# Last output layer of a fused attention and two-layer-MLP kernel: six of seven token tiles as seven block products

## The chip, the cores and the metric

The kernel runs on one core of a Trainium2 chip. The metric is the device time of one execution in microseconds (us). The three timed runs of the kernel before took 1274.81, 1283.0 and 1287.9 us, so the median is 1283.0 us. One more execution was taken with the hardware profiler; all rows below are from it.

## The reference

Everything is float32. Talking-heads attention is followed by two MLPs, and the second one is what the change touches:

```python
h = x @ w_in                                   # x: 1792 x 768, w_in: 768 x 2048
r = np.maximum(h, 0.0)
g = r * r                                      # 1792 x 2048
return (g @ w_out).astype(np.float32)          # w_out: 2048 x 768
```

The last output layer is the product `g @ w_out` for the second half of the tokens: 896 tokens, 2048 hidden features, 768 outputs.

## The kernel before

**Stages.** Attention writes its result in four token blocks of 448 to memory. Then the two MLPs run for two halves of 896 tokens each. The order of the stages in `run` is: first MLP of the first half (`inner(0)`, `outer_first`), second MLP of the first half (`inner(1)`, `outer_last(0)`), and then for the second half `seven(0)` (first input layer), `outer_combos` (first output layer), `seven(1)` (second input layer) and `outer_last(1)` (second output layer, the end of the program).

**How a float32 product is made.** Each operand is split into a high part (ScalarE casts it, `wh`, `xh`, `rh`, `eh`) and a low part (VectorE subtracts the high part from the operand, `wl`, `xl`, `rl`, `el`). `three` (L664 to L666) then issues three matmuls: high times high, high times low, low times high. L664 needs only the two high parts.

**Block products.** `seven` and the stages before it already use a scheme with seven block products where the plain one has eight: a 2x2 block matrix product is made from seven products of sums of blocks. In `seven` the sums of weights come from `combine` on VectorE, in products named b11, t1, b21, b22, t2, t3, t4. Eight groups `q` of seven products make the stage; `late` and `close` put the two last elementwise steps of a result some products later. `outer_last` does not use the scheme.

**outer_last(1).** h (the squared ReLU) lies in 16 tiles `hr` of 128 features by 896 tokens. For each of two halves `nh` of 384 outputs and each of 16 feature tiles `f` the stage takes one weight tile of 128x384 and issues `three` for seven token tiles: 2 x 16 x 7 x 3 = 672 matmuls with 384 moving columns, into seven PSUM banks. `split_ahead` splits a whole `hr` tile of 896 columns two steps ahead, in each half again (32 splits); `Weights.next` splits the weight tile of a step three steps ahead. After each half seven copies, by VectorE and ScalarE in turn, go to SBUF tiles `tmp` and are stored by SyncE.

**outer_combos.** Two passes `t` over 16 steps `f`. A step issues 18 matmuls of 448 columns. VectorE and ScalarE split one `hr` tile (L670, L669) and one weight tile (L525, L518) in a step. In the last three steps of a pass the matmuls are ordered by output tile, so that the results of the pass can be split while the matmuls still run.

**What sets the order.** The program is written out by hand: each engine runs its instructions in the order in which the Python code issues them, and a wait holds up everything behind it on that engine. All weight loads and stores are issued by SyncE in one such order. `Weights.units` is the list of weight tiles in order of use; `load_ahead` loads up to six tiles ahead into six buffers `wf` (four more are named `aq`), and `part` splits one tile into one of five buffer pairs `wh`, `wl`. The splits of h use four buffer pairs `rh`, `rl`. PSUM has eight banks, which `bank` hands out in turn.

Of the kernel before, what the change touches and what calls it, by code (L numbers as in the profile page):

```python
# [16 lines left out]
B, H, S, D = 4, 12, 448, 64  # L17
# [5 lines left out]
KC, FC = DM // 128, DFF // 128  # L23
WU = 448
FU = DM // 2
LINE = 256
MOVING, STATIONARY = 128, 224
# [354 lines left out]
class Weights:  # L382
# [180 lines left out]
def col(i):  # L563
    return slice(i * 128, (i + 1) * 128)


class Mlps:
    BLOCKS = [slice(j * S, (j + 1) * S) for j in range(2)]

    def __init__(self, tc, ctx, dram, psum, xd, weights, out):  # L570
        self.tc, self.nc, self.ctx, self.psum, self.xd, self.out = tc, tc.nc, ctx, psum, xd, out
        self.weights = Weights(tc.nc, dram, *weights)
        self.banks = 0
        self.pending = []
# [157 lines left out]
    def seven(self, m, x, carry=()):  # L732
# [23 lines left out]
        for q in range(FC // 2):  # L756
            a, b, c, d, e = (self.bank()[:, :S] for _ in range(5))
            plan = (("b11", a), ("t1", b), ("b21", a), ("b22", b), ("t2", c), ("t3", d), ("t4", e))
            for i, (name, p) in enumerate(plan):
# [81 lines left out]
    def outer_first(self, xh, xl, hh, hl):  # L841
        nc = self.nc
        for o in range(KC):
# [11 lines left out]
            for j, bl in enumerate(self.BLOCKS):  # L855
                self.split(xh[:, o, bl], xl[:, o, bl], p[j])

    def outer_combos(self):

        nc, tt, w = self.nc, self.nc.vector.tensor_tensor, self.weights  # L860
# [7 lines left out]
        for t in range(2):  # L868
            p = [[self.bank()[:, :S] for _ in self.BLOCKS] for _ in range(3)]
            taken = []  # L870
            for f in range(FC):
                s = t * FC + f
                tail = f >= FC - 3
# [61 lines left out]
    def outer_last(self, half):  # L935
# [27 lines left out]
                nc.sync.dma_start(out=self.out[r : r + 128, nh * n2 : (nh + 1) * n2], in_=o)  # L963
        return x if half == 0 else None

    def run(self):
        with ExitStack() as ctx:
            hp = self.pool("hp", "left", ctx)
# [19 lines left out]
        self.seven(0, x)  # L988
        x, carry = self.outer_combos()
        self.hr = {}  # L990
        self.start_split(STATIONARY)
        self.seven(1, x, carry)
        self.outer_last(1)


# ---- launch: one core; the host only lays the arrays out
# [46 lines left out]
```

## Time and profile before

| what | us |
|---|---|
| median of three timed runs (lowest, highest) | 1283.0 (1274.81, 1287.9) |
| time of the profiled execution | 1277.57 |
| its span, first to last instruction | 1275.7 |
| TensorE (PE) busy in the span | 1233.7 (97%) |
| VectorE (DVE) busy | 943.1 (74%) |
| ScalarE (ACT) busy | 679.3 (53%) |

In the rows below a time stamp is in us from the start of the span. In a row of the timeline the first number is the start, the second the duration of the instruction (or of all of them, where "xN" ends the row). A matmul's recorded duration overlaps the next one, so the pitch of matmuls is read from their starts. PEld is the weight load of TensorE, L12 is line 12 of the kernel, and square brackets give the idle time of the engine just before and the instruction that ended it.

### The profile page before, as it was taken

What the parts mean: (1) busy time and instruction counts of PE and PEld (TensorE: products, weight loads), DVE (VectorE), ACT (ScalarE), POOL (GpSimd) and SP (SyncE); (2) the same over time, 40 slices, a digit from 0 to 9 for tenths busy, and PEclk for the clock granted to TensorE, in tenths of its full rate; (3) what the DMA queues carried; (4) which work ended last, traced back from release to release, by engine and by line L of the source; (5) the groups of instructions that cost most, each with busy time, mean ns of one, the idle gap of its engine ahead of it and who ended that gap; (6) DMA issues with size and microseconds to landing.
All of it is one profiled execution on the core that took longest, in us unless ns stands there. A gap on an engine that the chain in (4) does not pass through costs nothing.

```text
span 1275.7 us, 35064 instructions
## 1 busy us (share of the span) xinstructions
PE 1233.7 (97%) x14295; PEld 1101.7 (86%) x14296; DVE 943.1 (74%) x1974; ACT 679.3 (53%) x1476; POOL 52.4 (4%) x118
## 2 busy tenths in 40 slices
PE   9999989999789999999999999999999999999998
PEld 4677777777579999988899999999999998999998
DVE  4577667777759998778999996868874559887452
ACT  4666666666537774333444554546663445454342
POOL 1011010110410000000000000000000000000000
PEclk9999999999999999999999999999999999999999
DMA  6666646555635545666666555131221111212131
GB/s 186 201 204 195 208 161 205 185 171 184 203 108 177 174 155 162 191 184 199 224 222 227 186 174 171 49 119 50 69 75 55 51 50 50 75 44 85 34 105 44
DMA packets 124121, 179.02 MB, mean 140 GB/s; under 512 B 25177, under 2 KB 103353, under 8 KB 123961
## 3 DMA queue, kind: packets, MB, share of 16 engines
q1 hardware_dynamic: 123720, 176.50, 43.0%
q8 instruction: 112, 1.84, 0.6%
q14 instruction: 49, 0.39, 0.1%
q10 hardware_dynamic: 240, 0.29, 0.1%
HBM read 101.86 MB, written 36.18 MB: 108 GB/s over the span
## 4 chain that ended last, share of the span: by engine, by line
PE 76%; DVE 11%; ACT 6%; DMA 3%; issue 3%; SPq 0%; ACTq 0%; DVEq 0%; POOL 0%; POOLq 0%
PE ps_qk L664 5%; PE ps_qk L666 5%; PE ps_qk L665 5%; PE ps_pv L665 5%; PE ps_pv L666 5%; PE ps_pv L664 5%; PE ps_post L664 5%; PE ps_post L666 5%; PE ps_post L665 5%; PE ps_mix L664 5%; PE ps_mix L666 5%; PE ps_mix L665 5%; PE ps_mix L182 4%; PE ps_post L218 4%; PE ps_pv L254 3%; PE ps_qk L156 3%
## 5 line engine op out<-in xcount | busy, mean ns | idle before, releaser
L518 ACT CAST wh<-wf 128x384 fp32r<-128x384 f32 (+1 forms) x272 | 133.3, 492 | 209.6 <-DVE wf L477 129.4
L525 DVE TENSOR_TENSOR wl<-wf,wh 128x384 fp32r<-128x384 f32 (+1 forms) x272 | 144.7, 534 | 76.4 <-ACT wh L518 74.7
L218 PEld LDWEIGHTS ps_post<-wg,ex 60*64 60x64 f32 x5040 | 139.5, 135 | 51.2 <-issue 30.2
L192 ACT ACTIVATE ex<-ps_mix,nmax 128x448 f32<-128x448 f32 x180 | 112.6, 630 | 117.5 <-DVE nmax L190 117.4
L670 DVE TENSOR_TENSOR rl<-hr,rh 128x896 fp32r<-128x896 f32 x96 | 104.5, 1089 | 54.4 <-ACT rh L669 54.4
L218 PE MATMUL ps_post<-wg,ex 60*64 60x60 f32 x5040 | 135.0, 220 | 6.5 <-issue 4.9
L236 DVE COPY at<-ps_post 128x420 f32<-128x420 f32 x178 | 97.6, 591 | 53.8 <-PE ps_post L218 51.1
L182 PE MATMUL ps_mix<-graw,pre 64*64 64x448 f32 (+1 forms) x720 | 113.6, 557 | 13.8 <-ACT ex L192 6.3
L190 DVE TENSOR_REDUCE nmax<-ps_mix 128x1 f32<-128x448 f32 x180 | 104.5, 616 | 24.3 <-PE ps_mix L182 23.9
L669 ACT CAST rh<-hr 128x896 fp32r<-128x896 f32 x96 | 90.1, 939 | 50.3 <-PE ps_post L666 25.1
L254 PE MATMUL ps_pv<-at,v 64*64 64x110 f32 (+3 forms) x2976 | 100.0, 249 | 5.3 <-issue 2.9
L254 PEld LDWEIGHTS ps_pv<-at,v 64*64 64x64 f32 x2976 | 88.4, 134 | 14.9 <-issue 6.5
L156 PE MATMUL ps_qk<-kt,qt 64*64 64x448 f32 (+1 forms) x680 | 92.6, 543 | 1.5 <-ACT sc L161 1.2
L447 ACT ACTIVATE wf<-wd 128x384 f32<-128x384 f32 (+1 forms) x134 | 68.1, 512 | 42.8 <-DMA wd<-w1o 24.0
L161 ACT COPY sc<-ps_qk 120x448 f32<-120x448 f32 x167 | 80.7, 539 | 11.1 <-PE ps_qk L156 11.1
L477 DVE SCALAR_TENSOR_TENSOR wf<-wd,wf 128x384 int32<-128x384 int32 (+1 forms) x134 | 67.7, 509 | 3.9
L475 DVE SCALAR_TENSOR_TENSOR wf<-wd,wf 128x384 int32<-128x384 int32 (+1 forms) x134 | 67.7, 509 | 3.8
L182 PEld LDWEIGHTS ps_mix<-graw,pre 64*64 64x64 f32 (+1 forms) x720 | 34.7, 134 | 32.7 <-ACT ex L192 16.6
L684 ACT ACTIVATE tmp<-tmp 128x448 f32<-128x448 f32 x48 | 27.9, 581 | 57.2 <-DVE tmp L794 43.9
L664 PE MATMUL ps_qk<-xh,wh 128*128 128x448 f32 x150 | 55.3, 369 | 0.3 <-DVE tmp L691 0.3
L666 PE MATMUL ps_qk<-xh,wl 128*128 128x448 f32 x150 | 55.0, 367 | 0.0
L665 PE MATMUL ps_qk<-xl,wh 128*128 128x448 f32 x150 | 55.0, 367 | 0.0
(247 smaller groups left out, 3152.1 us busy)
## 6 DMA issues: line engine op xcount, KB each, us to landing
graw<-sc SPq DMA_DIRECT2D x180, 210.0 KB
wd<-w1i SPq DMA_DIRECT2D x32, 384.0 KB
wd<-w1o SPq DMA_DIRECT2D x48, 256.0 KB
wd<-w2i SPq DMA_DIRECT2D x32, 384.0 KB
wf<-w2of SPq DMA_DIRECT2D x48, 192.0 KB
wd<-w2o SPq DMA_DIRECT2D x22, 384.0 KB
w1if<-wf SPq DMA_DIRECT2D x32, 192.0 KB
w1of<-wf SPq DMA_DIRECT2D x48, 128.0 KB
```

The costliest lines, as they stand in the source:

```text
L156: nc.tensor.matmul(out[a][x:y], qt[n][o, p, x:y], k[o, p, :], start=True, stop=True)
L182: nc.tensor.matmul(out[r][64 * g : 64 * g + 64], pre64[o], e[g][o], start=True, stop=True)
L190: nc.vector.tensor_reduce(nmax, p, AX.X, ALU.max, negate=True)
L192: nc.scalar.activation(e, p, AF.Exp, bias=nmax, scale=1.0, accum_out=tot[s][:, r : r + 1])
L218: nc.tensor.matmul(out[g][y, 6 if c == 3 else 2 * c + r], e[rows][o, key : key + 64], w[o, rows], start=True, stop=True)
L254: nc.tensor.matmul(p, vt[b, i // 3][y, jc, g % 6 * D : (g % 6 + 1) * D], m, start=(jc == 0), stop=(jc == JC - 1), skip_group_check=True)
L518: self.nc.scalar.copy(hi, f)
L525: self.nc.vector.tensor_tensor(lo, self.single.pop(i), hi.bitcast(F32), ALU.subtract)
L664: mm(p, wh, xh, start=first, stop=False)
L665: mm(p, wh, xl, start=False, stop=False)
L666: mm(p, wl, xh, start=False, stop=last)
L670: self.nc.vector.tensor_tensor(lo, raw, hi.bitcast(F32), ALU.subtract)
```

## The change

The end of the program, `outer_last(1)`, becomes `seven_last`.

- Of the seven token tiles, tiles 0 to 2 and 4 to 6 form the two row blocks; the 2048 features and the 768 outputs are cut into two blocks each. Seven products `n` of eight steps `f`, each with three token tiles, replace the plain ones. Token tile 3 is left out of the scheme: its two halves of outputs are accumulated beside products 0, 2 and 3 in two more banks (`rest`). A step has 15 matmuls in product 0, 12 in products 2 and 3 and 9 in products 1, 4, 5 and 6: 8 x (15 + 9 + 12 + 12 + 9 + 9 + 9) = 600 matmuls of 384 columns.
- The sums of h (`sums`, and in place in `hr`) are made by VectorE, one of 128x384 in each step of products 0 to 3, in the room of the tile `xh`. `part_last` splits 512 or 384 columns of one tile three steps ahead, 56 times. The first three splits lie in the last group of `seven(1)`, behind products 2, 4 and 6 of it; before, two splits of 896 columns lay behind products 2 and 4.
- The sums of weights are made in `outer_combos` by `sum_weights`: for each of eight feature tiles four loads of 128x384 by SyncE, four subtractions by VectorE (two in each of two steps, ahead of that step's splits), and four stores into a scratch tensor `w2ot`. Together that is 32 loads, 32 subtractions and 32 stores.
- The last stage takes 64 weight tiles instead of 32: 32 plain ones and 32 sums from the scratch. In a step it splits weight tiles until four are ready ahead.
- The results are combined after the products: six VectorE operations after each of products 4 and 5, three in product 6, plain copies elsewhere. The order of the last three steps of product 6 is by output tile.

```diff
@@ Weights: the list of tiles
-        self.units += kept
+        half = FC // 2
+        self.k2o, self.k2t = k2o, keep("w2ot", [4 * half, 128, FU])
+        place = {"b11": 0, "b21": half, "b12": FC, "b22": FC + half}
+        self.units += [("f32", k2o[place[x] + f], None, MOVING) for f in range(half) for x in ("b11", "b12")]
+        for x in ("t1", "b21", "b22", "t2", "t3", "t4"):
+            of = self.k2t[(int(x[1]) - 1) * half :] if x[0] == "t" else k2o[place[x] :]
+            self.units += [("f32", of[f], None, MOVING) for f in range(half)]
@@ seven
-                if q == FC // 2 - 1 and i in (2, 4):
-                    self.split_ahead(i // 4)
+                if q == FC // 2 - 1 and i in (2, 4, 6):
+                    if m == 0:
+                        if i < 6:
+                            self.split_ahead(i // 4)
+                    else:
+                        self.part_last(0, i // 2 - 1)
@@ new, called at the head of each step s of outer_combos
+    def sum_weights(self, s):
+        w, half, sub = self.weights, FC // 2, self.nc.vector.tensor_tensor
+        for j, at in enumerate((-1, 2, 4, 7, 10, 14, 18, 22)):
+            if s == max(at, 0):
+                self.four[j] = []
+                for x in (0, FC, half, FC + half):
+                    o = self.tmp()[:, :FU] if j in (1, 3) else w.plain("aq", 4)
+                    self.nc.sync.dma_start(out=o, in_=w.k2o[x + j])
+                    self.four[j].append(o)
+            if s == at + 2:
+                b11, b12, b21, b22 = self.four[j]
+                sub(b11, b12, b11, ALU.subtract)
+                sub(b12, b22, b12, ALU.subtract)
+            if s == at + 3:
+                b11, b12, b21, b22 = self.four.pop(j)
+                sub(b22, b22, b11, ALU.subtract)
+                sub(b21, b22, b21, ALU.subtract)
+                for i, o in enumerate((b11, b22, b12, b21)):
+                    self.nc.sync.dma_start(out=w.k2t[i * half + j], in_=o)
@@ new
+    def part_last(self, n, f):
+        a = (STATIONARY - H_AT) % LINE // 4
+        t = self.sums[f] if n in (1, 4) else self.hr[f + (FC // 2 if n in (2, 3, 6) else 0)]
+        t = t[:, 512:] if n == 6 else t[:, : 512 if n in (0, 2, 3) else 384]
+        parts = [self.hq.tile([128, 2 * S + LINE // 4], F32R, name=f"r{x}", bufs=4)[:, a : a + t.shape[1]] for x in "hl"]
+        self.split(*parts, t)
+        self.halves[n, f] = parts
@@ new, in place of outer_last(1); the core of its loop
+        for k, (n, f) in enumerate(steps):
+            w.load_ahead(w.used)
+            hi, lo = self.halves.pop((n, f))
+            if f == 0 and n in (1, 4, 5, 6):
+                banks.append([self.bank()[:, :FU] for _ in range(3)])
+            p = banks[(0, 1, 0, 1, 2, 3, 4)[n]]
...
+            if not tail:
+                for i in range(3):
+                    for g, hi, lo, weights in taken:
+                        self.three(p[i], hi[:, col(i)], lo[:, col(i)], *weights[0], n not in (2, 3) and g == 0,
+                                   n in (2, 3, 4, 5, 6) and g == half - 1, True)
...
+                if n in (0, 2, 3):
+                    for j, y in enumerate(weights):
+                        q = j if n == 0 else n - 2
+                        self.three(rest[q], hi[:, col(3)], lo[:, col(3)], *y, n == 0 and f == 0, n > 0 and f == half - 1, True)
...
+            while w.done < min(len(w.units), w.used + 4):
+                w.part()
+            if k + 3 < len(steps):
+                self.part_last(*steps[k + 3])
+            low, high = self.hr[f], self.hr[f + half]
+            if n == 0:
+                tt(self.sums[f], low[:, 512:], high[:, 512:], ALU.add)
+            elif n == 1:
+                tt(self.sums[f], self.sums[f], low[:, :FU], ALU.subtract)
+            elif n == 2:
+                tt(high[:, :FU], high[:, :FU], self.sums[f], ALU.subtract)
+            elif n == 3:
+                tt(low[:, :FU], low[:, :FU], low[:, 512:], ALU.subtract)
...
+                elif n == 4:
+                    tt(u[i], p[i], one_a[i], ALU.add)
+                    o = room()
+                    tt(o, both[i], u[i], ALU.add)
+                    put(o, i, 1)
```

Line numbers move with the change: L669 and L670 (the splits) become L675 and L676, L518 and L525 (the parts of weights) L524 and L531, L664 to L666 (the matmuls) L670 to L672.

Two places on VectorE matter below. The first is where the two passes of `outer_combos` meet. Rows of before; `xl` is the low part of a result of the first pass, `rl` that of an h tile for the second pass, `wl` that of a weight tile:

```order
L670 TENSOR_TENSOR xl<-ps_mix,xh 128x448
L889 TENSOR_TENSOR tmp<-tmp,ps_mix 128x448
L670 TENSOR_TENSOR xl<-tmp,xh 128x448
L670 TENSOR_TENSOR rl<-hr,rh 128x896 x2
L525 TENSOR_TENSOR wl<-wf,wh 128x384 x2
L670 TENSOR_TENSOR rl<-hr,rh 128x896
```

The same place in the change; `aq` are the weight tiles that are subtracted:

```order
L676 TENSOR_TENSOR xl<-ps_mix,xh 128x448
L921 TENSOR_TENSOR tmp<-tmp,ps_mix 128x448
L676 TENSOR_TENSOR xl<-tmp,xh 128x448
L880 TENSOR_TENSOR aq<-aq 128x384
L881 TENSOR_TENSOR aq<-aq 128x384
L676 TENSOR_TENSOR rl<-hr,rh 128x896 x2
L531 TENSOR_TENSOR wl<-wf,wh 128x384 x2
L884 TENSOR_TENSOR aq<-aq 128x384
L885 TENSOR_TENSOR aq<-aq 128x384
L676 TENSOR_TENSOR rl<-hr,rh 128x896
```

Two subtractions now stand between the last split of a result and the first split of h for the second pass, and two more behind the weight parts.

The second place is where `seven(1)` ends and the last stage begins. Rows of before; L793 to L801 and L753 combine the products of the last group, L693 squares the ReLU:

```order
L670 TENSOR_TENSOR rl<-hr,rh 128x896
L793 TENSOR_TENSOR tmp<-ps_post,tmp 128x448
L794 TENSOR_TENSOR tmp<-ps_mix,tmp 128x448
L525 TENSOR_TENSOR wl<-wf,wh 128x384
L800 TENSOR_TENSOR tmp<-ps_pv,tmp 128x448
L801 TENSOR_TENSOR tmp<-tmp 128x448
L525 TENSOR_TENSOR wl<-wf,wh 128x384
L753 TENSOR_TENSOR tmp<-tmp,ps_qk 128x448
L693 TENSOR_TENSOR hr<-tmp 128x448 x3
L525 TENSOR_TENSOR wl<-wf,wh 128x384 x2
L670 TENSOR_TENSOR rl<-hr,rh 128x896
```

The same place in the change (L799 to L807, L759 and L699 are the same lines as L793 to L801, L753 and L693); the row with L1069 is the first sum of h:

```order
L676 TENSOR_TENSOR rl<-hr,rh 128x512
L799 TENSOR_TENSOR tmp<-ps_post,tmp 128x448
L800 TENSOR_TENSOR tmp<-ps_mix,tmp 128x448
L531 TENSOR_TENSOR wl<-wf,wh 128x384
L806 TENSOR_TENSOR tmp<-ps_pv,tmp 128x448
L807 TENSOR_TENSOR tmp<-tmp 128x448
L531 TENSOR_TENSOR wl<-wf,wh 128x384
L676 TENSOR_TENSOR rl<-hr,rh 128x512
L759 TENSOR_TENSOR tmp<-tmp,ps_qk 128x448
L699 TENSOR_TENSOR hr<-tmp 128x448 x2
```

A split of 512 columns now stands ahead of L759. Behind the rows shown follow one more L699, four weight parts instead of two, a split of 512 columns and L1069.

## Rows read from the trace of the kernel before

**Rows 1.** The page's first line: span of the profiled execution.

```profile
span 1275.7 us, 35064 instructions
```

**Rows 2.** Windows of the last three stages: length, then busy us by engine (instructions), clock, DMA.

```profile
core 0: us, PE busy (x) PEld busy (x) DVE busy (x) ACT busy (x) POOL busy (x), PEclk, DMA share, GB/s
937.40:1053.00 115.60, 115.55 (x579) 108.10 (x578) 63.63 (x92) 53.35 (x86) 0.00 (x0) 1.00 0.20 59
1053.00:1155.20 102.20, 101.30 (x505) 94.36 (x504) 89.04 (x168) 53.82 (x111) 0.00 (x0) 1.00 0.19 59
1155.20:1272.00 116.80, 116.67 (x673) 116.34 (x672) 55.30 (x74) 44.20 (x68) 0.00 (x0) 1.00 0.20 62
```

**Rows 3.** Waits of TensorE from 830 us on: us in total, times, longest.

```profile
PE ps_mix L664 <- ACT tmp L775: 0.5, 1, 0.5
PE ps_post L664 <- ACT tmp L780: 0.4, 1, 0.4
```

**Rows 4.** Timeline, TensorE: end of the stage before, first and last matmul of the last stage.

```profile
1151.43 0.36 PE L666 MATMUL ps_post<-eh,wl 128*128 128x448 f32 x1
...
1155.03 0.36 PE L666 MATMUL ps_qk<-eh,wl 128*128 128x448 f32 x1
1155.23 0.34 PE L664 MATMUL ps_mix<-wh,rh 128*128 128x384 f32 x1
...
1271.53 0.34 PE L666 MATMUL ps_post<-wh,rl 128*128 128x384 f32 x1
```

**Rows 5.** Timeline, VectorE, where the last stage begins.

```profile
1151.36 1.08 DVE L670 TENSOR_TENSOR rl<-hr,rh 128x896 fp32r<-128x896 f32 x1
1152.37 0.61 DVE L793 TENSOR_TENSOR tmp<-ps_post,tmp 128x448 f32<-128x448 f32 x1
...
1155.68 0.61 DVE L753 TENSOR_TENSOR tmp<-tmp,ps_qk 128x448 f32<-128x448 f32 x1
1156.21 1.69 DVE L693 TENSOR_TENSOR hr<-tmp 128x448 f32<-128x448 f32 x3
1157.82 1.02 DVE L525 TENSOR_TENSOR wl<-wf,wh 128x384 fp32r<-128x384 f32 x2
```

**Rows 6.** Timeline, ScalarE, same place.

```profile
1155.33 0.58 ACT L684 ACTIVATE tmp<-tmp 128x448 f32<-128x448 f32 x1 [0.68 <-DVE tmp L801]
1156.33 0.58 ACT L684 ACTIVATE tmp<-tmp 128x448 f32<-128x448 f32 x1 [0.42 <-DVE tmp L753]
1156.81 0.91 ACT L518 CAST wh<-wf 128x384 fp32r<-128x384 f32 x2
1157.63 0.94 ACT L669 CAST rh<-hr 128x896 fp32r<-128x896 f32 x1
```

**Rows 7.** Timeline, where the two passes of outer_combos meet: VectorE, ScalarE and TensorE.

```profile
996.95 1.78 ACT L669 CAST rh<-hr 128x896 fp32r<-128x896 f32 x2
...
997.08 0.62 DVE L670 TENSOR_TENSOR xl<-tmp,xh 128x448 fp32r<-128x448 f32 x1 [0.63 <-ACT xh L669]
...
997.92 2.09 DVE L670 TENSOR_TENSOR rl<-hr,rh 128x896 fp32r<-128x896 f32 x2 [0.22 <-ACT rh L669]
...
998.65 0.36 PE L664 MATMUL ps_pv<-rh,wh 128*128 128x448 f32 x1
999.07 0.47 PE L665 MATMUL ps_pv<-rl,wh 128*128 128x448 f32 x1
```

**Rows 8.** Timeline, VectorE, a step within outer_combos, then within the last stage.

```profile
1032.55 1.09 DVE L670 TENSOR_TENSOR rl<-hr,rh 128x896 fp32r<-128x896 f32 x1 [2.04 <-ACT rh L669]
1033.56 0.55 DVE L525 TENSOR_TENSOR wl<-wf,wh 128x384 fp32r<-128x384 f32 x1
...
1228.77 0.56 DVE L525 TENSOR_TENSOR wl<-wf,wh 128x384 fp32r<-128x384 f32 x1 [1.70 <-ACT wh L518]
```

**Rows 9.** Timeline, SyncE: the weight loads of outer_combos.

```profile
918.54 97.91 SPq L425 DMA_DIRECT2D wf<-w1of  x32
```

**Rows 10.** Timeline, end of the program: VectorE.

```profile
1271.91 0.56 DVE L961 COPY tmp<-ps_post 128x384 f32<-128x384 f32 x1 [0.48 <-PE ps_post L666]
```

More of the change, by code (lines that the diff above doesn't have):

```diff
@@ L573, in __init__ @@
         self.banks = 0
-        self.pending = []
+        self.pending, self.four = [], {}
     def pool(self, name, side, ctx=None):
@@ L872, in outer_combos @@
                 s = t * FC + f
+                self.sum_weights(s)
                 tail = f >= FC - 3
@@ L964, in outer_last, with seven_last, rooms, put @@
         return x if half == 0 else None
+    def part_last(self, n, f):
[5 more added lines that the diff above has]
+        self.halves[n, f] = parts
+    def seven_last(self):
+        nc, w = self.nc, self.weights
+        copy, tt, half = nc.scalar.copy, nc.vector.tensor_tensor, FC // 2
+        def rooms(pool, tag, n):
+            room = pool.tile([128, n], F32, name=tag, tag=tag)
+            return [room[:, i * FU : (i + 1) * FU] for i in range(n // FU)]
+        high = rooms(self.xp, "xh", KC * 2 * S + LINE // 4)
+        self.sums = high[:half]
+        kept = [rooms(self.ep, f"e{x}", 9 * S) for x in "hl"]
+        one_a, one_b, both, u = kept[0][:3], kept[0][3:6], kept[0][6:9], kept[1][:3]
+        def put(o, i, nh):
+            r = 2 * S + i * 128
+            nc.sync.dma_start(out=self.out[r : r + 128, nh * FU : (nh + 1) * FU], in_=o)
+        def room():
+            return self.tmp()[:, :FU]
+        def out(p, i, nh, engine):
+            o = room()
+            engine(o, p)
+            put(o, i, nh)
+        copies = nc.vector.tensor_copy, copy
+        steps = [(n, f) for n in range(7) for f in range(half)]
+        banks = [[self.bank()[:, :FU] for _ in range(3)]]
+        rest = [self.bank()[:, :FU] for _ in range(2)]
+        taken = []
+        for k, (n, f) in enumerate(steps):
[5 more added lines that the diff above has]
+            if n == 0:
+                weights = [w.take(), w.take()]
+            else:
+                weights = [w.take()]
+            taken.append((f, hi, lo, weights))
+            tail = n == 6 and half - 3 <= f < half - 1
+            if not tail:
[3 more added lines that the diff above has]
+                                   n in (2, 3, 4, 5, 6) and g == half - 1, True)
+                    if n == 6 and f == half - 1:
+                        o = room()
+                        tt(o, u[i], p[i], ALU.subtract)
+                        put(o, 4 + i, 0)
+                if n in (0, 2, 3):
+                    for j, y in enumerate(weights):
+                        q = j if n == 0 else n - 2
+                        self.three(rest[q], hi[:, col(3)], lo[:, col(3)], *y, n == 0 and f == 0, n > 0 and f == half - 1, True)
+                taken.clear()
+            while w.done < min(len(w.units), w.used + 4):
[3 more added lines that the diff above has]
+            low, high = self.hr[f], self.hr[f + half]
+            if n == 0:
+                tt(self.sums[f], low[:, 512:], high[:, 512:], ALU.add)
[5 more added lines that the diff above has]
+                tt(low[:, :FU], low[:, :FU], low[:, 512:], ALU.subtract)
+            if f < half - 1:
+                continue
+            for i in range(3):
+                if n == 0:
+                    copy(one_a[i], p[i])
+                elif n == 1:
+                    copy(one_b[i], p[i])
+                elif n == 2:
+                    out(p[i], i, 0, copies[i % 2])
+                elif n == 3:
+                    copy(both[i], p[i])
+                elif n == 4:
+                    tt(u[i], p[i], one_a[i], ALU.add)
+                    o = room()
+                    tt(o, both[i], u[i], ALU.add)
+                    put(o, i, 1)
+                elif n == 5:
+                    tt(u[i], p[i], u[i], ALU.add)
+                    o = room()
+                    tt(o, u[i], one_b[i], ALU.add)
+                    put(o, 4 + i, 1)
+            if n in (2, 3):
+                out(rest[n - 2], 3, n - 2, copies[n - 2])
@@ L990, in run @@
         self.hr = {}
-        self.start_split(STATIONARY)
+        self.halves = {}
         self.seven(1, x, carry)
-        self.outer_last(1)
+        self.seven_last()
 def kernel(q, k, v, w_pre, w_post, moe_w_in, moe_w_out, moe2_w_in, moe2_w_out):
```

## The prediction, made before the changed kernel ran

> **What bounds the kernel now.** I read the windows by stage first. TensorE is busy in 115.55 of 115.60 us in outer_combos, in 101.30 of 102.20 us in seven(1), and without a gap in the last stage [rows 2]; from 830 us on its waits sum to 0.9 us [rows 3]. So the end of the program is a queue of matmuls, and a matmul that is taken out there shortens it by its pitch. VectorE is far below that in the last stage (55.30 of 116.80 us) but not in seven(1) (89.04 of 102.20) [rows 2]. The timeline then says at which places VectorE is only just in time; those decide what the added VectorE work costs.
>
> **The matmuls taken out.** The last stage starts its first matmul at 1155.23 and its 672nd at 1271.53 [rows 4], a pitch of 116.30 / 671 = 0.1733 us. The change issues 600 matmuls of the same form. 72 x 0.1733 = **12.48 us** less, if TensorE never waits.
>
> **Durations for the added work.** A VectorE operation of 128x384 lasts 0.55 us, but two in a row take 1.02, so the second starts 0.47 behind the first [rows 5]. For 448 columns that pitch is 0.53 (1155.68 to 1156.21) and for 896 it is about 1.0 (two in 2.09) [rows 5, 7]. No row has 512 columns; between 384 and 896 I take 0.60 on VectorE, bounds 0.47 and 1.0. For ScalarE's cast the rows are about 0.5 at 384 (two in 0.91) and 0.94 at 896 [rows 6]; at 512 I take 0.62, bounds 0.5 and 0.94.
>
> **Sums of weights in outer_combos.** Most of the 32 subtractions are hidden: a step of 18 matmuls of 448 columns lasts 18 x 0.20 = 3.6 us there (pitch from 1155.03 to 1155.23 [rows 4]), and VectorE idles 2.04 us of it ahead of the split of h [rows 8], while two subtractions want 0.94. One pair is not hidden. Where the two passes meet, VectorE ends the low part of a result begun at 997.08 and starts the split of the next h tile at 997.92; TensorE issues the high-high matmul at 998.65 and then has to wait for that split until 999.07, where 998.85 was due [rows 7]. The change puts two subtractions between these two VectorE instructions. The split then starts at 997.08 + 0.53 + 2 x 0.47 = 998.55 instead of 997.92, so TensorE waits 0.63 us longer. Two more subtractions follow the second split, but the split behind them is due two steps (7.2 us) later. Bounds: 0.6 at the pitch, 0.9 if nothing overlaps (0.62 + 2 x 0.55 = 1.72, against 0.84 now). I take **0.63 us**.
>
> The stores of the sums stand in SyncE's one queue, ahead of weight loads, and wait for VectorE's subtractions. Before, the 32 loads of this stage are issued from 918.54 to 1016.45 [rows 9], far ahead of their use in a stage that ends at 1053 [rows 2]. In the change a load behind the stores of step s fetches the tile that is split three steps later: 10.8 us for the issue of four stores and, where buffers `aq` are used again, the landing of a store and of a load. A landing costs at most 3.2 us: the last copy ends at 1272.47 [rows 10], and its store is done when the span ends at 1275.7 [rows 1]. Two of them leave 4.4 us of cover, so I cost this at nothing.
>
> **The start of the last stage.** This is the largest loss. At its first matmul (1155.23) VectorE still has to finish the last results of seven(1): L753 at 1155.68, three squarings, and only then the low parts of the next weight tiles, at 1157.82 [rows 5]. Before, that was in time, since the second step began 21 matmuls (3.64 us) after the first. In the change the first step has 15 matmuls, so the second step's second matmul, which needs such a low part, is due at 1155.23 + 16 x 0.1733 = 1158.00. And the split of 512 columns ahead of L753 has to wait for ScalarE's cast, which stands behind the ReLU at 1155.33 [rows 6].
> - VectorE comes to L793 earlier, since two splits of 896 became 512 (2 x 0.4 less). Its product's last matmul starts at 1151.43 and ends at 1151.79 [rows 4], against 1152.37 now [rows 5]: 0.5 us earlier. So the ReLU comes at about 1154.85.
> - The cast follows 0.48 later (1156.33 to 1156.81 in [rows 6]) and ends at 1154.85 + 0.48 + 0.62 = 1155.95. The split starts at 1156.0, L753 at 1156.6.
> - From L753 to the first weight part it is 2.14 us (1155.68 to 1157.82) [rows 5]: 1158.74, ending at 1159.29. TensorE's matmul comes at about 1159.35 instead of 1158.00.
>
> That is **1.35 us**. With the 384-column prices it is 1.1; with those of 896 columns and no earlier start it is 2.5. After it the weight tiles of the next step follow at a pitch of 0.47, and TensorE needs the next one 12 matmuls (2.1 us) later.
>
> **The rest of the last stage.** A step of product 0 lasts 15 x 0.1733 = 2.60 us and asks VectorE for two weight parts, one split of 512 and one sum: 2 x 0.47 + 0.60 + 0.47 = 2.01. Product 1: 1.56 us, against 3 x 0.47 = 1.41. Products 2 and 3: 2.08, against 1.54. Products 4 to 6: 1.56, against 0.94. ScalarE has less. So VectorE keeps up, and splits run three steps ahead. After products 4 and 5 six operations on results take 3.2 us (three pairs, a dependent pair 0.58 + 0.47), inside the three steps (4.7 us) of lead. The stores of these results hold up weight loads in SyncE's queue; the third store leaves after VectorE's part and split of that step (1.5 us) and the 3.2 us, so the load behind it leaves some 5 us after the step began. With a landing of 2 us the weight part and the split behind it on VectorE are ready 0.8 us ahead of need, with 3.2 us they are 0.4 us late. I take nothing, with 0.4 us at each of the two places as the upper end. The end of the program keeps its form: one VectorE operation of 0.56 us and a store [rows 10].
>
> **Sum.** 12.48 - 0.63 - 1.35 = **10.5 us** less. The profiled execution took 1277.57 us with a span of 1275.7 [rows 1], so it would become 1267.1. That execution is faster than the median of the timed runs, 1283.0; on that base, which I take, it is 1283.0 - 10.5 = **1272.5 us**, 0.8% less.
>
> **A rule against the row.** Two neighbours of 0.55 us each ended after 1.02 us [rows 5], so the pitch is 0.47. The Trainium skill, VectorE: DVE Perf Modes, section on the DRAIN you can't avoid, says that the next VectorE operation does not start until the pipe is empty. By that rule each added operation costs its full 0.55: the first loss becomes 0.9, the second 1.35 + 5 x 0.08 = 1.75, and the sum 9.8. The row decides here, and I keep 10.5.
>
> **Rivals.**
> - *TensorE hardly waits (saving 11.5 to 12.5, 1271).* If ScalarE casts for the new split before L753's operand is there, the second loss shrinks to what four weight parts need. For it speaks that L753 is free to start only when seven(1)'s last matmul, begun at 1155.03 [rows 4], has ended; against it, that the weight part must follow L753 and three squarings in any case.
> - *VectorE becomes the bound in the last stage (saving about 6, 1277).* Without overlap product 1 asks for 3 x 0.55 = 1.65 us in steps of 1.56; with each hand-over from ScalarE exposed as it is now (1.70 us of VectorE's idle time is waiting for the weight cast [rows 8]), VectorE lags some 0.2 to 0.4 us a step through 16 steps, beyond the lead of 4.7 us at the ends of products. I price it at 4 to 5 us. Against it: those waits are there because VectorE is early.
> - *SyncE's queue (slower, 1285 or more).* The stores of the sums wait for VectorE, and weight loads queue behind them, eight times in outer_combos. It decides the sign from 10.5 / 8 = 1.3 us of wait each time on. With 1.5 us more than that each it is 12 us lost, 1285 to 1295. Against it speaks the cover of 4.4 us above.
>
> **How the numbers follow.** Chances: the forecast 0.62, the first rival 0.15, the second 0.19, the third 0.04. About 1% is what a measurement of this kernel can tell from no change: three runs lie 13 us apart. A saving of 1% is 12.8 us, more than the 12.5 that the matmuls can give, so faster by over 1% comes only with scatter of the runs: 0.3 of the forecast's cases, 0.5 of the first rival's, 0.15 of the second's, together 0.29. Slower by over 1% is most of the third, 0.03. The range goes from 1262 (the first rival, in runs as far below the median as the lowest now, 8 us) to 1282 (the second, in runs as far above it as the highest, 5 us).
>
> **What would show it.** TensorE has 600 matmuls in the last stage at a pitch of 0.173; a wait of about 0.8 us for `rl` (L676) where the passes of outer_combos meet; a wait of about 1.3 us for `wl` (L531) in the second step of the last stage; no other new wait. If the second step starts without a wait, the chain was wrong. If waits for `rl` or `wl` repeat through products 1 to 6, VectorE or the loads are the bound. If TensorE waits in outer_combos for weight parts, it is SyncE's queue.

## The result, and the profile of the changed kernel

The changed kernel takes 1267.0 us (median; 1264.1 to 1269.9) against 1282.2 for the kernel before on the same chip (1274.8 to 1287.9): a ratio of 0.988, interval 0.983 to 0.992. The forecast was 1272.5, and 10.5 us less. In a second comparison with more rounds (experiment 1) it is 1270.0 against 1279.6, a ratio of 0.992 (0.990 to 0.995). The two comparisons agree within their intervals; the gain is 15.2 us by the medians of the first and 9.6 by those of the second, and by the first pair of traces some 10 us of it come from the change (below).

The changed kernel's first line, and two of its windows: outer_combos and the last stage, each from its first matmul. The columns are those of [rows 2].

```profile
span 1262.3 us, 35367 instructions
```

```profile
934.10:1050.50 116.40, 115.59 (x579) 108.16 (x578) 79.80 (x124) 53.50 (x86) 0.00 (x0) 1.00 0.50 163
...
1152.60:1259.00 106.40, 105.15 (x602) 103.92 (x600) 86.54 (x171) 59.76 (x129) 0.00 (x0) 1.00 0.42 131
```

Beside [rows 2] the last stage has 600 matmuls instead of 672 and is 10.4 us shorter by these windows. VectorE now works 86.54 of its 106.40 us there, where it worked 55.30 of 116.80; in outer_combos it works 79.80 us instead of 63.63, and the DMA share rises from 0.20 to 0.50, the sums of weights with their loads and stores. TensorE is still busy nearly throughout. Its waits from 930 us on (us in total, times, longest), to be laid beside [rows 3]:

```profile
PE ps_pv L671 <- DVE rl L676: 0.8, 1, 0.8
PE ps_mix L671 <- DVE wl L531: 0.6, 1, 0.6
PE ps_mix L670 <- ACT tmp L781: 0.5, 1, 0.5
PE ps_post L670 <- ACT tmp L786: 0.4, 1, 0.4
PE ps_mix L670 <- ACT wh L524: 0.4, 1, 0.4
```

The third and fourth were there before. The first is the border of the two passes of outer_combos; the second and the last are the start of the last stage. Nothing else is new in this view.

**Where the time went.** Three marks divide the end of a trace: the first matmul of outer_combos, the first of the last stage, and the start of the last matmul. With them the time from the start of outer_combos to the end is 338.25 us in the profiled execution before (1275.7 - 937.45) and 328.14 in the changed kernel's (1262.3 - 934.16): 10.1 us less. In parts: outer_combos with seven(1) 217.78 and 218.54 us (0.76 more), the last stage from its first matmul to the start of its last 116.30 and 105.77 (10.53 less), and what lies behind that 4.17 and 3.83 (0.34 less). The remaining 3.3 us of the difference between the two spans lie ahead of outer_combos, where the two kernels have the same instructions. Over the ten traces of this study, of eight kernels with one program up to there, outer_combos starts anywhere from 932 to 951 us. So the marks behind it measure the change better than the spans do. They are not free of scatter either: the second pair of traces gives 8.6 us (experiment 1).

### The profile page after: what moved, and what is told of

It is laid out like the page before. It is cut to its first block, busy times and chain, and to the rows that moved or that the text cites. A ratio compares the mean times of both kernels' runs of the same rounds, so it can differ in the third digit from the quotient of the medians.

```text
span 1262.3 us, 35367 instructions
## 1 busy us (share of the span) xinstructions
PE 1220.5 (97%) x14223; PEld 1088.2 (86%) x14224; DVE 990.5 (78%) x2104; ACT 695.6 (55%) x1537; POOL 52.5 (4%) x118
## 4 chain that ended last, share of the span: by engine, by line
PE 78%; DVE 11%; ACT 6%; issue 3%; DMA 1%; SPq 0%; ACTq 0%; DVEq 0%
PE ps_qk L670 5%; PE ps_qk L671 5%; PE ps_qk L672 5%; PE ps_pv L672 5%; PE ps_pv L671 5%; PE ps_post L670 5%; PE ps_mix L672 5%; PE ps_pv L670 5%; PE ps_mix L671 5%; PE ps_post L672 5%; PE ps_post L671 5%; PE ps_mix L670 5%; PE ps_mix L182 4%; PE ps_post L218 4%; PE ps_pv L254 4%; PE ps_qk L156 3%
## 5 line engine op out<-in xcount | busy, mean ns | idle before, releaser
L524 ACT CAST wh<-wf 128x384 fp32r<-128x384 f32 (+1 forms) x304 | 149.6, 494 | 196.9 <-DVE wf L483 129.0
L531 DVE TENSOR_TENSOR wl<-wf,wh 128x384 fp32r<-128x384 f32 (+1 forms) x304 | 162.4, 537 | 53.5 <-ACT wh L524 51.8
L676 DVE TENSOR_TENSOR rl<-hr,rh 128x896 fp32r<-128x896 f32 (+2 forms) x104 | 94.8, 914 | 25.6 <-ACT rh L675 25.6
L675 ACT CAST rh<-hr 128x896 fp32r<-128x896 f32 (+2 forms) x104 | 82.9, 799 | 48.6 <-PE ps_post L672 24.7
L670 PE MATMUL ps_qk<-xh,wh 128*128 128x448 f32 x150 | 55.3, 369 | 0.0
L672 PE MATMUL ps_qk<-xh,wl 128*128 128x448 f32 x150 | 54.9, 366 | 0.0
```

What stands on the lines that cost most here:

```text
L524: self.nc.scalar.copy(hi, f)
L531: self.nc.vector.tensor_tensor(lo, self.single.pop(i), hi.bitcast(F32), ALU.subtract)
L670: mm(p, wh, xh, start=first, stop=False)
L672: mm(p, wl, xh, start=False, stop=last)
```

## The experiments

In all experiments "start to end" is the time from the first matmul of outer_combos to the end of the span, 338.25 us before. Experiments 2, 4 and 5 are one traced execution each and are read by the marks. The edits are shown as parts of diffs; the names are those of the change's diff.

### 1. How large is the gain? Both kernels again, five rounds

The changed kernel, and the kernel before against itself, unchanged.

> The changed kernel, timed again. From its first matmul of outer_combos to the end of the span its trace took 328.1 us, the one of before 338.3: 10.1 us less. The other 3.3 us of its gain (934.2 against 937.5 us) lie ahead of outer_combos, where no instruction differs. Theory: those are scatter of the runs; five more rounds give a ratio near 0.992 (10.1 of 1278), and the time to the start of outer_combos differs as much between traces of one kernel as between the two kernels. Rival: the change makes the earlier stages faster too (by where its instructions or tiles lie); then the ratio is again near 0.988, and outer_combos starts some 3 us earlier in each trace of the changed kernel than in each of the kernel before.

> The kernel before, unchanged, timed against itself: the ratio is 1.000, and the width of its interval is what the rounds can tell. Theory (scatter): the start of outer_combos moves by some us against the 937.5 us of the first trace. Rival (the change speeds up earlier stages): it stays within 1 us of 937.5. From there to the end of the span it takes 338.3 us as before, within 0.3.

The changed kernel came to 1269.98 us (1263.6 to 1273.4, 12 runs) against 1279.62 (29 runs of the kernel before): a ratio of 0.9924, interval 0.9895 to 0.9953. 10.1 us of 1279.6 would be 0.9921. The kernel before against itself gave 0.9999 (0.9969 to 1.0029). So the 15.2 us between the medians of the first comparison, four runs each, were the 10 us that the marks show and scatter of runs; a difference of 0.3% is about what five rounds can tell.

The traces speak against the rival: outer_combos starts at 937.45 and 932.04 us in the two traces of the kernel before, at 934.16 and 934.63 in those of the changed one, so it moves more within one kernel than between the two. One expectation was missed. Start to end is not 338.3 us in the second trace of the kernel before but 1274.9 - 932.04 = 342.86, and in the second of the changed kernel 1268.9 - 934.63 = 334.27: 8.6 us less, not 10.1. In both the matmuls follow more slowly for a long stretch (last section). Outer_combos with seven(1) differs as in the first pair (222.43 and 223.18 us, 0.75 more), but in the changed kernel the slower pace goes on through the last stage, which takes 107.27 us instead of 105.77. Without these 1.5 us the second pair, too, would give 10.1; that is an estimate.

### 2. The sums of weights alone

The kernel before, with the sums made in outer_combos and stored by the change's own `sum_weights`, and the last stage as it was. The scratch is written and read by nothing.

```diff
+        self.k2o, self.k2t = k2o, keep("w2ot", [4 * half, 128, FU])
...
+    def sum_weights(self, s):
...
+                self.sum_weights(s)
```

> The kernel before with only the sums of weights added in outer_combos (32 loads, 32 subtractions, 32 stores into a scratch that nothing reads); the last layer is the plain one. Theory: one thing changes, the wait where the two passes meet: the gap between the high-high and the next matmul there, 0.42 us before, becomes 1.17 as in the changed kernel; from the start of outer_combos to the end of the span 338.3 + 0.75 = 339.0 us. Rival (SyncE's queue or the extra traffic costs time elsewhere in outer_combos): other waits for weight parts, 340 us or more.

Start to end is 1285.2 - 946.22 = 338.98 us, 0.73 more than before. Its waits of TensorE from 930 us on:

```profile
PE ps_pv L667 <- DVE rl L672: 0.8, 1, 0.8
PE ps_mix L666 <- ACT tmp L777: 0.5, 1, 0.5
PE ps_post L666 <- ACT tmp L782: 0.4, 1, 0.4
```

One new wait, at the border. So 32 loads, 32 subtractions and 32 stores cost 0.7 us altogether, and all of it at the one place where VectorE had nothing to spare.

### 3. All losses taken away

The changed kernel with three edits: the group of sums whose first subtractions stand at the border is moved one step later; the split of 512 columns ahead of L759 is moved behind the weight parts of the last stage's first step; and the stores of products 4 and 5 are issued three steps later, behind the weight loads of those steps.

```diff
-        for j, at in enumerate((-1, 2, 4, 7, 10, 14, 18, 22)):
+        for j, at in enumerate((-1, 2, 4, 7, 10, 15, 18, 22)):
...
-                    else:
+                    elif i < 6:
                         self.part_last(0, i // 2 - 1)
...
                 w.part()
+            if k == 0:
+                self.part_last(0, 2)
...
-                    put(o, i, 1)
+                    hold(o, i, 1)      # put() at step k + 3, behind w.load_ahead
```

> The changed kernel with its three waits taken away by order alone: the sums of the sixth feature tile one step later (15 in place of 14), so that no subtraction stands where the passes meet; the third split of the last layer moved from ahead of L759 to behind the four weight parts of the first step; the stores of products 4 and 5 issued three steps later, behind the weight loads. Theory: the gaps of 1.17, of 0.70 and 1.07, and of 0.41 us become 0.42, about 0.2 and 0.2 each in excess of none, and 0.17; from the start of outer_combos to the end of the span 328.1 - 0.75 - 1.3 - 0.3 = 325.8 us; no output differs. The ratio to before is then about 0.990 if the gain ahead of outer_combos was scatter, 0.986 if not. Rival: the waits move to the next instruction in line and less than 1 us comes back.

Start to end is 1264.7 - 938.92 = 325.78 us: 12.5 less than before and 2.4 less than the change. By parts: 217.84, 104.11 and 3.83. Its waits of TensorE from 930 us on are the two that the kernel before had:

```profile
PE ps_mix L670 <- ACT tmp L781: 0.5, 1, 0.5
PE ps_post L670 <- ACT tmp L786: 0.4, 1, 0.4
```

and at the start of the last stage the timeline of TensorE (start, duration, operation) shows what is left there:

```profile
1159.36 0.34 PE L670 MATMUL ps_mix<-wh,rh 128*128 128x384 f32 x1
1159.71 0.44 PE L671 MATMUL ps_mix<-wl,rh 128*128 128x384 f32 x1
1159.99 0.34 PE L672 MATMUL ps_mix<-wh,rl 128*128 128x384 f32 x1
```

The steps from start to start of 0.35 and 0.28 are 0.29 us above the pitch of 0.173, where the change loses 1.54 (below). The gap at the border is 0.43 us again, as before the change, and the one at the end of product 5 is gone. Timed, this kernel takes 1266.31 us (1258.0 to 1274.2, 12 runs), a ratio of 0.9900 to the kernel before (0.9866 to 0.9933). It is the fastest of the study by median; its 2.4 us over the change stand in the marks, while the intervals of the two ratios overlap.

### 4. How much room has VectorE in the last stage? One more operation in each step

The changed kernel with one additional sum of 128x384 in each of the 48 steps of products 1 to 6, and then with two. The results of the additional sums are read by nothing.

```diff
                 tt(low[:, :FU], low[:, :FU], low[:, 512:], ALU.subtract)
+            if n > 0:
+                tt(kept[1][4], self.hr[f][:, :FU], self.hr[f][:, 384:768], ALU.add)
```

> The changed kernel with one more VectorE operation of 128x384 in each step of products 1 to 6 (48 in all; its output is read by nothing). Theory (VectorE keeps up, splits run three steps ahead): VectorE then asks for 1.88 us in steps of 1.56 (product 1), 2.01 in 2.08 (products 2 and 3) and 1.41 in 1.56 (products 4 to 6), so that it falls behind by 2.5 us in product 1 and by 3.2 us at the end of products 4 and 5, against a lead of 4.7 us. TensorE waits 1 to 3 us more in the last stage, near the ends of products 4 and 5. Rival (VectorE is the bound already, or lags 0.2 to 0.4 us a step): each added operation shows, 48 x 0.47 = 22 us or more.

The last stage grows from 105.77 to 114.62 us: 8.9 us for 48 x 0.47 = 22.6 us of VectorE work. That is neither the few us of the one theory nor the whole of the other. The largest waits of TensorE from 925 us on:

```profile
PE ps_pv L672 <- DVE rl L676: 2.6, 2, 2.0
PE ps_qk L672 <- DVE rl L676: 1.7, 1, 1.7
```

Single waits of 1.7 and 2.0 us stand in the fourth steps of products 5 and 6, for the first splits behind the operations on the results of products 4 and 5. That is where the theory had put them, but they are larger; the rest that the view lists are waits of 0.2 to 0.6. By the starts of the products' first matmuls, beside those of the change, nothing is lost in product 1, 0.1 us in product 2, 1.2 in product 3, 1.2 in product 4, 2.5 in product 5 and 3.9 in product 6. VectorE's windows in this kernel (length, busy us, instructions, clock, DMA share, GB/s) show why:

```profile
1190.00:1206.00 16.00, 16.00 (x34) 1.00 0.36 100
...
1238.00:1254.00 16.00, 15.90 (x35) 1.00 0.33 101
```

VectorE runs without a pause from 1190 to 1206 us and nearly so from 1238 to 1254; in the change it worked 86.54 us in the whole stage of 106.40. In product 1 it is asked for 4 x 0.47 = 1.88 us in steps of 1.56 and falls 8 x 0.32 = 2.6 us behind; in products 2 and 3 (1.54 + 0.47 = 2.01 in steps of 2.08) the theory lets it win back 16 x 0.07 = 1.1. The timeline shows two things that this leaves out. Behind product 2 VectorE copies three results (L1029, 1218.67 to 1220.07, 1.4 us). And in product 3 the added sum reads the tile that the sum ahead of it has just written: it starts 0.58 us behind it (1221.14 and 1221.72) instead of 0.47, so that a step asks for 2.13 us, more than its 2.08. So TensorE waits from product 3 on, and VectorE comes to the 3.2 us of operations on results behind product 4 without the three steps of lead that the theory counted on.

> The same with two more VectorE operations in each step of products 1 to 6 (96 in all). Theory: VectorE is the bound from product 1 on, with 2.35 us in steps of 1.56, 2.48 in 2.08 and 1.88 in 1.56: behind by 6.3 + 6.4 + 7.7 us, and 7.8 us of work on results, less the lead of 4.7: 20 to 24 us more in the last stage. Rival (VectorE is the bound already): 96 x 0.47 = 45 us more.

With two the last stage lasts 132.92 us, 27.2 more than in the change, where 20 to 24 were expected; the second operation costs 18.3 us of its 22.6. Some 1.5 us of the 27.2 are a lower clock behind a wait (last section). The window of that stage, columns as in [rows 2]:

```profile
1174.00:1306.80 132.80, 116.72 (x600) 103.39 (x599) 128.10 (x264) 59.88 (x129) 0.00 (x0) 0.99 0.33 102
```

VectorE is busy in 128.10 of 132.80 us: it is the bound now. So in the change it is not, but its room is small: one operation of 0.47 us in each step takes it up.

### 5. How much cover has SyncE's queue? The stores of the sums twice, and four times

The same four tiles are stored to the same place again, so that only time on the queue and traffic are added.

```diff
-                for i, o in enumerate((b11, b22, b12, b21)):
+                for i, o in 2 * list(enumerate((b11, b22, b12, b21))):
                     self.nc.sync.dma_start(out=w.k2t[i * half + j], in_=o)
```

> The changed kernel with each store of a sum of weights issued twice: 32 more stores on SyncE, ahead of weight loads. In the trace of the changed kernel four stores take 3.8 to 5.3 us on SyncE, so a group holds the loads behind it some 4.7 us longer. Theory (cover of 4.4 us by the prediction's count): at most 0.4 us of wait at each of eight groups, 0 to 3 us in outer_combos. Rival (SyncE's queue has no cover): 8 x 4.7 = 38 us.

Outer_combos with seven(1) takes 221.10 us, 2.56 more than in the change. TensorE has two new waits of about 1 us, for a split of h:

```profile
PE ps_mix L671 <- DVE rl L676: 2.0, 2, 1.1
```

The timeline of VectorE just ahead of them (the brackets give the idle time before and what ended it):

```profile
987.11 0.56 DVE L880 TENSOR_TENSOR aq<-aq 128x384 f32<-128x384 f32 x1 [3.14 <-DMA aq<-w2of]
989.27 0.56 DVE L881 TENSOR_TENSOR aq<-aq 128x384 f32<-128x384 f32 x1 [1.59 <-DMA aq<-w2of]
989.74 1.08 DVE L676 TENSOR_TENSOR rl<-hr,rh 128x896 fp32r<-128x896 f32 x1
```

The loads that came late are those of the tiles to be subtracted: SyncE issues them behind the eight stores of the group before. The subtractions wait for them on VectorE, and the split of h, which needs no such load, waits behind the subtractions. In the changed kernel such subtractions already wait at one place, the first of the pair for 0.20 us and the second for 0.48, and it costs nothing:

```profile
963.34 0.56 DVE L881 TENSOR_TENSOR tmp<-tmp 128x384 f32<-128x384 f32 x1 [0.48 <-DMA tmp<-w2of]
964.14 1.09 DVE L676 TENSOR_TENSOR rl<-hr,rh 128x896 fp32r<-128x896 f32 x1 [0.24 <-ACT rh L675]
```

The split behind them comes when ScalarE's cast is there, 0.24 us after VectorE was free.

> The changed kernel with each store of a sum of weights issued four times: some 19 us of SyncE's time for each of eight groups, where the groups lie 7 to 14 us apart. Theory: SyncE becomes the bound of outer_combos, since 8 x 19 us for stores and 8 x 4 to 5 us for loads are more than its 115 us; 40 to 80 us more in that stage, in waits for weight parts. If stores that wait for nothing new leave faster than that, it is less: at 0.45 us each (the pitch of loads) 16 stores take 7 us and there is no wait to see.

Outer_combos with seven(1) takes 244.56 us, 26.0 more than in the change, less than the 40 to 80 expected. The place was missed too: none of the waits is for a weight part of outer_combos, and the largest are, as with the stores doubled, for the split of h behind the subtractions. And the queue was faster than the 19 us counted for a group: 16 stores take 9.1 to 12.6 us on SyncE. The largest of TensorE's waits from 930 us on:

```profile
PE ps_mix L671 <- DVE rl L676: 14.8, 3, 8.8
PE ps_pv L671 <- DVE rl L676: 3.2, 3, 1.5
```

The waits for the split of h make 18.0 us, 0.8 of them also in the change. Some of the rest of the 26.0 is lost behind them, to a lower clock (last section).

## Why the prediction was right

The bound was read rightly: matmuls taken out of a queue of matmuls shorten it by their pitch, and the losses sit where VectorE was only just in time. The terms, one by one.

**The matmuls taken out.** 12.48 us forecast. With the losses taken away the whole end is 12.5 us shorter than before (experiment 3). The last stage alone is 116.30 - 104.11 = 12.19 shorter there, and the 0.29 at its start that remains makes the sum 12.48.

**The border of the two passes.** 0.63 forecast. Timeline of VectorE, then of TensorE, in the changed kernel, as in [rows 7]:

```profile
994.32 0.55 DVE L880 TENSOR_TENSOR aq<-aq 128x384 f32<-128x384 f32 x1
994.91 0.56 DVE L881 TENSOR_TENSOR aq<-aq 128x384 f32<-128x384 f32 x1
995.39 1.08 DVE L676 TENSOR_TENSOR rl<-hr,rh 128x896 fp32r<-128x896 f32 x1
```

```profile
995.36 0.36 PE L670 MATMUL ps_pv<-rh,wh 128*128 128x448 f32 x1
996.53 0.47 PE L671 MATMUL ps_pv<-rl,wh 128*128 128x448 f32 x1 [0.81 <-DVE rl L676]
```

From start to start the two matmuls are 1.17 us apart, 0.42 before [rows 7]: 0.75 us lost. The forecast let both subtractions follow at the pitch of 0.47. The second subtracts with the first one's result, so it starts 0.59 behind it, the pitch of the dependent pair that the prediction used elsewhere (0.58): 0.12 us more, which is the whole miss. By experiment 2 nothing else of the sums of weights costs time.

**The start of the last stage.** 1.35 forecast. VectorE, ScalarE and TensorE in the changed kernel, as in [rows 4 to 6]:

```profile
1153.54 0.69 DVE L676 TENSOR_TENSOR rl<-hr,rh 128x512 fp32r<-128x512 f32 x1 [0.69 <-ACT rh L675]
1154.15 0.61 DVE L759 TENSOR_TENSOR tmp<-tmp,ps_qk 128x448 f32<-128x448 f32 x1
1154.68 1.69 DVE L699 TENSOR_TENSOR hr<-tmp 128x448 f32<-128x448 f32 x3
1156.28 1.96 DVE L531 TENSOR_TENSOR wl<-wf,wh 128x384 fp32r<-128x384 f32 x4
```

```profile
1152.42 0.58 ACT L690 ACTIVATE tmp<-tmp 128x448 f32<-128x448 f32 x1 [0.82 <-DVE tmp L807]
1152.90 0.60 ACT L675 CAST rh<-hr 128x512 fp32r<-128x512 f32 x1
1154.79 0.58 ACT L690 ACTIVATE tmp<-tmp 128x448 f32<-128x448 f32 x1 [1.29 <-DVE tmp L759]
1155.28 1.73 ACT L524 CAST wh<-wf 128x384 fp32r<-128x384 f32 x4
```

```profile
1152.70 0.34 PE L670 MATMUL ps_mix<-wh,rh 128*128 128x384 f32 x1
...
1155.12 0.34 PE L672 MATMUL ps_mix<-wh,rl 128*128 128x384 f32 x1
1155.82 0.44 PE L670 MATMUL ps_mix<-wh,rh 128*128 128x384 f32 x1 [0.36 <-ACT wh L524]
1156.89 0.45 PE L671 MATMUL ps_mix<-wl,rh 128*128 128x384 f32 x1 [0.62 <-DVE wl L531]
1157.18 0.34 PE L672 MATMUL ps_mix<-wh,rl 128*128 128x384 f32 x1
```

The chain is the one forecast, instruction by instruction. Counted from the stage's first matmul (1155.23 before, 1152.70 now) the ReLU comes at -0.28 (forecast -0.38), L759 at +1.45 (+1.37), the first weight part at +3.58 (+3.51), and the matmul that needs it at +4.19 (+4.12). Each is 0.07 to 0.1 later than forecast, and all of that is in the ReLU. The prices that no row of before had came out as taken: ScalarE's cast of 512 columns 0.60 us (0.62 taken), VectorE's split 0.69 with L759 0.61 behind it (a pitch of 0.60 taken). One thing was missed: the wait is in two parts, since the high part comes late too (the wait for `wh`, which begins at 1155.28 behind the ReLU at 1154.79), and a third step from start to start of 0.29 follows. So the waits that the view shows are 0.36 and 0.62 us, where one of about 1.3 had been named as the sign. The three, 0.70, 1.07 and 0.29, are 1.54 us above the pitch.

A dependent pair starts 0.59 apart, while independent neighbours keep the pitch of 0.47: four weight parts take 1.96 us here, 3 x 0.47 + 0.55. The Trainium skill, VectorE: DVE Perf Modes, section on the DRAIN you can't avoid, says that the next operation does not start until the pipe is empty, and goes on that one which is not held starts earlier. The first sentence fits the pair here and the second the four. The prediction took only the first as the rule, and the sum of 9.8 us that it drew from it rests on half of what the section says; no run here shows what holds an operation.

**The ends of products 4 and 5.** Nothing taken, 0.4 us each as the upper end. At the end of product 4 TensorE does not wait. At the end of product 5 it does:

```profile
1254.25 0.34 PE L671 MATMUL ps_pv<-wl,rh 128*128 128x384 f32 x1
1254.66 0.44 PE L672 MATMUL ps_pv<-wh,rl 128*128 128x384 f32 x1
1254.94 0.34 PE L670 MATMUL ps_pv<-wh,rh 128*128 128x384 f32 x1
```

0.41 and 0.28 instead of 0.173 each: 0.35 us, the upper end. SyncE's timeline and then ScalarE's show the way that was named:

```profile
1247.06 2.45 SPq L1022 DMA_DIRECT2D out<-tmp  x3
1249.61 0.87 SPq L431 DMA_DIRECT2D wf<-w2ot  x2
```

```profile
1252.10 0.52 ACT L524 CAST wh<-wf 128x384 fp32r<-128x384 f32 x1 [3.65 <-DMA wf<-w2ot]
```

The stores hold the loads back until 1249.61, and ScalarE's cast waits for the weights until 1252.10, 2.5 us after the issue; the landing was near the middle of the bounds taken (2 to 3.2). In experiment 3, with these stores issued later, this gap is gone. The way is right, but that the size meets the upper end is luck: by the count of the prediction (0.8 us to spare with a landing of 2 us, 0.4 late with 3.2) a landing of 2.5 leaves 0.3 to spare. What made the split late is the order of the last three steps of product 6 by output tile, which that count left out: the matmul at 1254.66, the first that needs the low part of step 7's tile, stands six matmuls (1.04 us) earlier than in the plain order. VectorE's row of that split and the next:

```profile
1254.06 1.02 DVE L676 TENSOR_TENSOR rl<-hr,rh 128x384 fp32r<-128x384 f32 x2
```

The first ends at 1254.61. The matmul was due at 1254.42, and in the plain order at 1255.46. Product 5 keeps the plain order, and behind product 4 there is no gap.

**The end of the program.** Taken as unchanged; what lies behind the start of the last matmul is 0.34 us shorter (4.17 and 3.83). Every trace with the old last stage has 4.12 to 4.17 there, every one with the new one 3.80 to 4.02. The last VectorE operation is no shorter, so it is in the last store; which property of it was not tried.

**The sum.** The last stage loses 1.54 and 0.35 us and the border 0.75, the end gives 0.34: 12.48 - 1.54 - 0.35 - 0.75 + 0.34 = 10.18, against 10.11 by the marks and 10.5 forecast. That the sum is met within 0.4 us is in part luck: the losses came to 2.64 us instead of 1.98, and half of the difference was made up by the 0.34 at the end that nobody had forecast. The time of 1272.5 was 5.5 us above the first comparison and 2.5 above the second (1270.0). Runs scatter by that much: the kernel before, taken at 1283.0, has since come to 1282.2 and 1279.6, and the changed kernel to 1267.0 and 1270.0.

**The rivals.** *TensorE hardly waits* is not so: it loses 2.6 us, where 2.0 were forecast. *VectorE becomes the bound* is not so in the change, but it was given the reason that counts (product 1), and it is nearer than the count of steps said: with one more operation a step TensorE waits from product 3 on, and the three steps of lead are gone when the operations on the results of products 4 and 5 come (experiment 4). *SyncE's queue* is a real mechanism that this change does not reach. The step of the prediction that was wrong there is the place: it followed a weight load behind the stores to its own use and counted 4.4 us of cover. The first to be late are the loads of the sums themselves, with the subtraction waiting on VectorE and the split of h behind it (experiment 5). In the changed kernel such a subtraction waits 0.48 us already; with the stores doubled it costs 2.6 us in all.

## What to carry to other kernels

Where one engine runs without a gap, price removed work at its pitch, and look for losses only at the places where another engine is just in time: there were three. Two came out to within 0.2 us from rows of before, and the third at the end of its bounds, by an order of matmuls that had not been counted. Work added to an in-order engine is free where it idles and costs its pitch where it does not, 0.47 us for independent operations of 128x384 and 0.59 from the first to the second of a dependent pair here; moving three pieces of it (one step later, behind more urgent work, behind the next loads) got 2.4 us back at no cost that the trace shows. A load that feeds added work is more dangerous than it looks when that work stands ahead of something urgent on its engine: follow what queues behind the waiting instruction, not only the load's own use.

## What the runs showed of the hardware

**A slower pace at full granted clock.** In the second traces of both kernels, and in that with two additional operations, the matmuls of 448 columns follow at 0.207 us instead of 0.200, while the granted clock reads 1.00. In all three this begins within 1 us behind TensorE's wait where the passes of outer_combos meet (at 994, 997 and 1013 us; the other seven traces have a wait there too, without the slower pace), pauses for 3 to 5 us where seven(1) begins, and lasts to the start of the last stage. In the second trace of the changed kernel it takes hold again behind the waits at the start of that stage: 72 matmuls of 384 columns (product 1) take 12.72 us there, 12.48 in the first trace. Two windows, of the second trace of the kernel before and of the changed kernel's first:

```profile
1060.00:1150.00 90.00, 90.00 (x437) 81.42 (x437) 74.84 (x142) 46.53 (x93) 0.00 (x0) 1.00 0.19 59
```

```profile
1060.00:1150.00 90.00, 90.00 (x452) 84.48 (x451) 76.97 (x146) 45.82 (x95) 0.00 (x0) 1.00 0.22 67
```

437 matmuls in 90 us instead of 452, with TensorE busy throughout in both. It comes with either kernel and is worth about 4.6 us in outer_combos and seven(1) (222.43 us in the second trace of the kernel before, 217.78 in the first), so it is part of the scatter between runs. Its cause is open.

**The clock after a long wait.** With the stores fourfold TensorE once waits 8.8 us. Windows around it, columns as in [rows 2]:

```profile
976.00:985.80 9.80, 1.01 (x6) 0.61 (x4) 2.15 (x4) 1.12 (x2) 0.00 (x0) 0.67 0.94 319
985.80:989.50 3.70, 3.68 (x10) 3.29 (x11) 3.67 (x6) 1.90 (x4) 0.00 (x0) 0.50 0.54 191
989.50:996.00 6.50, 6.50 (x33) 5.90 (x32) 0.74 (x2) 0.94 (x1) 0.00 (x0) 0.99 1.03 352
```

TensorE had run six matmuls in the 9.8 us before; then the granted clock is 0.50, the lower level of 1.2 GHz, and ten matmuls take 3.7 us, after which it is back at 0.99. The same comes behind a wait of 5.0 us in that trace (0.53 in the 5.6 us that follow). Ten matmuls at 0.37 instead of 0.20 are 1.7 us that no wait shows. A shorter wait can do it too. With two operations added to each step (experiment 4) TensorE twice waits 3.2 us; behind the first the granted clock reads 1.00 and behind the second:

```profile
1296.60:1301.20 4.60, 4.58 (x17) 4.58 (x18) 4.60 (x11) 2.16 (x5) 0.00 (x0) 0.63 0.42 125
```

Ten matmuls of 384 columns follow at 0.32 us there instead of 0.173, some 1.5 us. The change's own waits, 0.8 us at most, leave the clock at 1.00 in each of its windows.
